# Attention with a threshold, then an MLP: the division by the softmax sums moves behind the value product, the first pairs are turned by plain transposes, and eight blocks of the MLP instead of six go through seven products of quarters

## The chip, the core and the metric

The kernel runs on one core of a Trainium2 chip. The core has a matrix engine (TensorE, PE in the profile, with its weight loads as PEld), a vector engine (VectorE, DVE), an engine for activation functions (ScalarE, ACT), GpSimd (POOL) and SyncE (SP), which here only issues transfers. Each engine works through its own list of instructions in order. Transfers are issued from SP's and POOL's lists and carried by 16 DMA engines. The metric is the device time of one execution in microseconds (us); lower is better.

## What is computed

```python
scale = 1.0 / np.sqrt(q.shape[-1])                       # q, k, v: (8, 8, 576, 64)
scores = scale * np.matmul(q, k.transpose(0, 1, 3, 2))
thresh = np.max(scores, axis=-1, keepdims=True) - tau
scores = np.where(scores >= thresh, scores, -1000000000.0)
scores = scores - np.max(scores, axis=-1, keepdims=True)
attn = np.exp(scores)
attn = attn / (np.sum(attn, axis=-1, keepdims=True) + 1e-09)
attn_out = np.matmul(attn, v)
x = attn_out.transpose(0, 2, 1, 3).reshape(8 * 576, 8 * 64)   # (4608, 512)
h = x @ w_in                                              # w_in: (512, 2048), float64
g = 0.5 * h * (1.0 + erf(h / sqrt(2)))
out = g @ w_out                                           # w_out: (2048, 512), float64
```

Everything is done in float32; the two weight matrices arrive as float64 and are converted on the chip.

## The kernel before

**Pairs, chunks and slots.** Heads are taken in pairs (e = 0, 1): 8 batches x 4 pairs are 32 pairs. The 576 rows of a head's scores are 4 chunks of 128 and a tail of 64; the tails of the two heads share a fifth chunk. One chunk of one pair is a *slot*, so a pair has five slots, i = 0 to 4, and there are 160 slots, listed in `slots` and walked by the loop at the end of the kernel. The instructions of all engines are issued in the order in which this loop calls the steps; nothing reorders them later.

**One slot.** `scores` (L345) computes 128x576 scores per head into PSUM (tile `sc`, two buffers, so each slot waits until the one before has been used). `softmax_head` takes the negated maxima (L356, DVE), the exponentials (L357, ACT) and the thresholds (L360). `softmax_tail` multiplies by "score is at least the threshold" and sums the row in one instruction (L370), adds 1e-9 and takes the reciprocal (L374, L375). For the pairs from the fifth on it then divides the weights themselves (L386 on DVE, now and then L384 on ACT).

**Turning the weights.** The value product needs the weights transposed (tile `pT`, one buffer for each of the two heads). The first four pairs (`EARLY`) use TensorE: a matmul with a diagonal matrix `diag` that holds the reciprocals (L291, made on ACT at L379), so that turning and dividing are one step. All later pairs use 32x32 transposes on DVE (`turn_p`, L398, into `pd`, or `pd_tail` in slot 4), and transfers on SP's queue put the 32x32 blocks in their places in `pT` (`regroup`): eight in slot 2 and eight in slot 3 (L413), four for the tails in slot 4 (L409).

**The value product.** `weigh_v` (L424) multiplies `pT` by `v` in two halves of 288 columns and gives 128 rows of x^T for the pair; ACT copies them from PSUM to the blocks of x^T (L433). For the later pairs it is called in slot 2 (`WEIGH`) of the next pair, between that slot's scores and its share of the MLP. The first four pairs go in two rounds (chunks 0 and 1 of all four, then chunks 2 to 4) and have it two slots after their last chunk of the round.

**The MLP.** Tokens go in 18 blocks of 256. Twelve blocks are *plain*: `block_steps` issues 64 matmuls with w_in (L473), gelus on ACT (L453), 32 matmuls with w_out (L485), the copy (L488) and the store. These are cut in small steps, and `fill` puts them behind the other steps of each slot, as many as a plan says: `GOAL` is how many blocks are to be done by which slot, and `PARTS` shares this among the five slots of a pair. The last six blocks go in three pairs (`DUOS`) through seven products of quarters in place of eight (`strassen`, matmuls at L591), after all attention work. The blocks' x^T wait in the pool `xg`; one of them (`AWAY`) is put into DRAM meanwhile (`put_away`) and fetched back (`bring`).

**Loads.** q, k and v of a pair are loaded about two pairs ahead, on SP for the first pairs and on POOL afterwards (L215, L223). In the first stage SP also loads the first pairs' q, k and v (L233 to L247). The weights are loaded by POOL in pieces, and four DVE instructions and one ACT instruction convert each piece (`conversions`, L172 to L183), between the slots' other work.

Of the kernel before, what the change touches and what calls it, by code (L numbers as in the profile page):

```python
# [18 lines left out]
def kernel(  # L19
# [28 lines left out]
    nc = tc.nc  # L48
# [19 lines left out]
    PLAIN = N_BLK - 6  # L68

    DUOS = [(n, n + 1) for n in range(PLAIN + 1, N_BLK - 1, 2)] + [(N_BLK - 1, PLAIN)]  # L70
    AWAY = [PLAIN]
# [12 lines left out]
    gp = ctx.enter_context(tc.tile_pool(name="gp", bufs=N_DF // 2 + 3))  # L84
    dg = ctx.enter_context(tc.tile_pool(name="dg", bufs=1))
# [9 lines left out]
    pd = [const.tile([P, 4 * KR, P], FP32, name=f"pd{e}") for e in range(2)]  # L95
    pd_tail = [const.tile([P, 4 * KR, Q], FP32, name=f"pd_tail{i}") for i in range(2)]
# [184 lines left out]
    def turn_p_early(p, i):  # L281


# [3 lines left out]
        w, diag = s.pop(("p", i)), s.pop(("diag", i))  # L287
        n = 1 if i == NC else 2

        def turn(to, cols, e):  # L290
            nc.tensor.matmul(to, lhsT=w[:, cols], rhs=diag[:, e, :], start=True, stop=True)  # L291

        for e in range(n):
            tr = ps.tile([P, NC, P], FP32, tag="mm", name="tr")
            for c in range(NC):
                at = e * (S + TAIL) + c * P
                turn(tr[:, c, :], slice(at, at + P), e)
            if i < NC:
                nc.scalar.copy(s["pT"][e][:, 0:NC, i * P:(i + 1) * P], tr)
# [5 lines left out]
        if i < NC:  # L305
            for e in range(2):
                at = MAIN + e * TAIL
                turn(tr[e * TAIL:(e + 1) * TAIL, 0, :], slice(at, at + TAIL), e)
            nc.scalar.copy(tails[:, i * P:(i + 1) * P], tr[:, 0, :])
            return  # L310
        turn(tr[0:TAIL, 0, :], slice(MAIN, S), 0)
# [50 lines left out]
    def softmax_tail(p, i, early, shared):  # L362

        s = st[p]
        sc, thr, w = s.pop(("sc", i)), s.pop(("thr", i)), s["p", i]
        n = len(sc)
        den = small.tile([P, 2], FP32, tag="den", name="den")
        for e in range(n):
            row = w[:, e * S:(e + 1) * S].rearrange("p (h s) -> p h s", h=2)
            nc.vector.scalar_tensor_tensor(  # L370
                row, sc[e][:, :, 0:HALF], thr[:, e:e + 1], row, op0=ALU.is_ge, op1=ALU.mult,
                accum_out=den[:, e:e + 1])
        rden = small.tile([P, 2], FP32, tag="rden", name="rden")
        nc.vector.tensor_scalar(den[:, 0:n], den[:, 0:n], 1e-9, None, op0=ALU.add)  # L374
        nc.vector.reciprocal(rden[:, 0:n], den[:, 0:n])  # L375
        if early:
            diag = s["diag", i] = dg.tile([P, 2, P], FP32, tag="diag", name="diag")
            for e in range(n):
                nc.scalar.activation(diag[:, e, :], ident, AF.Copy, bias=0.0, scale=rden[:, e:e + 1])  # L379
            return  # L380
        for e in reversed(range(n)):
            row = w[:, e * S:(e + 1) * S]
            if e == 0 and n == 2 and shared:
                nc.scalar.activation(row, row, AF.Copy, bias=0.0, scale=rden[:, e:e + 1])  # L384
            else:
                nc.vector.tensor_scalar(row, row, rden[:, e:e + 1], None, op0=ALU.mult)  # L386
# [28 lines left out]
    def weigh_v(p, lo, hi):  # L415

        b, hp = divmod(p, HP)
# [9 lines left out]
        at = lo  # L427
        while at < hi:
            n, o = divmod(b * S + at, TOK)
            size = min(TOK - o, hi - at)  # L430
            if n not in x_blk:
                x_blk[n] = xg.tile([P, N_DM, TOK], FP32, tag="x", name="x")
            nc.scalar.copy(x_blk[n][:, hp, o:o + size], xT[:, at - lo:at - lo + size])  # L433
            at += size
        if hi == S:
            del st[p]

# [122 lines left out]
    def strassen(ext, room):  # L560
# [9 lines left out]
        room += [x for _ in range(N_DF // 2 + 3) for x in unit(gp, "g")]  # L570
        room += [u for t in pd for u in units(t)]
        room += [x for e in range(2) for x in unit(one, f"pT{e}", 5)]

        def quarter():
            got = [room.pop(0).rearrange("p (j t) -> p j t", t=TOK) for _ in range(NJ // 2)]
            return lambda j: got[j // 2][:, j % 2, :]
# [143 lines left out]
    GOAL += [(BATCH * (m + 2) + WEIGH, x) for m, x in enumerate([1.96, 3.63, 5.31, 6.98, 8.65, 10.33, PLAIN])]  # L720
# [8 lines left out]
    PARTS = (1.36, 1.36, 0.5, 1.36, 0.42), (1.25, 1.25, 0.55, 1.25, 0.7)  # L729
# [4 lines left out]
    for n in range(len(slots) + WEIGH + 1):  # L734
        p, i = slots[n] if n < len(slots) else divmod(n, SLOTS)
        batch = n // BATCH
# [7 lines left out]
        busy = len(late)  # L744
# [3 lines left out]
        for args in due:  # L748
            weigh_v(*args)
        due = []  # L750
        if p > EARLY and i == WEIGH:
            for h in range(2):
                weigh_v(p - 1, h * HALF, (h + 1) * HALF)
        owed += (goal(n) - goal(n - 1)) * BLK_NS * (PARTS[n > 2 * BATCH + WEIGH][i] if not early and p < NP else 1.0)
# [6 lines left out]
        if p < NP:  # L761

            softmax_tail(p, i, early, batch == 1 and not busy)
            if not early:
                turn_p(p, i)
                if i == 2:
                    regroup(p, 1)
                if i > 2:
                    regroup(p, i)
# [72 lines left out]
```

## Time and profile before

| What | Value |
|---|---|
| time, median of 3 runs | 1446.6 us (1445.63 to 1447.43) |
| the profiled execution's own time | 1442.53 us |
| its span, first to last instruction | 1440.8 us, mean granted TensorE clock 0.992 |
| busy: PE, PEld, DVE, ACT, POOL | 1392.3, 943.3, 1036.7, 661.7, 291.2 us |
| chain that ended last, by engine | PE 84%, DVE 8%, ACT 5%, DMA 1%, issue 1% |
| DMA queue of SP (`q1`), share of 16 engines | 39.8% |
| DMA queue of POOL (`q0`), share of 16 engines | 15.0% |
| first stage (four early pairs, conversion) | 0 to about 170 us |
| pairs 4 to 31 with plain blocks between | about 170 to 1145 us |
| three pairs of blocks by seven products | 1145 to 1440.8 us |

A profile is one execution, so its rows add up to 1440.8 us and not to the median. Busy time counts an instruction from its start to its end; matmuls overlap, so the time from one start to the next tells more of PE than the mean duration. A float32 matmul has two records in the trace, a plain transpose one. An engine that is idle costs nothing unless something on the path to the end waits for it.

### The profile page before, as it was taken

The page shows a single profiled execution, that of the slowest core. Times are in us where ns is not written, and L with a number is a line of the kernel's source. Part 1 is how long each engine was busy: PE and PEld are TensorE (multiplying, and loading weights), DVE is VectorE, ACT ScalarE, POOL GpSimd, SP SyncE. Part 2 cuts the span into 40 slices and gives each one's busy share as a digit, 9 for nine tenths or more (in the row PEclk, how much of TensorE's full clock was granted, in tenths as well). Part 3 has the DMA queues.
Part 4 walks back from the last instruction along what each step waited for, and adds up shares of the span by engine and source line. Part 5 has one row for each costly group of instructions (what it writes and reads, how often), then busy time and mean ns, then how long its engine had stood idle before and what let it go on. Part 6 is the DMA issues. An engine that isn't in the chain of part 4 may idle for free.

```text
span 1440.8 us, 19431 instructions
## 1 busy us (share of the span) xinstructions
PE 1392.3 (97%) x6480; PEld 943.3 (65%) x6480; DVE 1036.7 (72%) x2344; ACT 661.7 (46%) x1122; POOL 291.2 (20%) x502
## 2 busy tenths in 40 slices
PE   6899989999999999999999999999999999999999
PEld 5576546556474656657475565756556588888887
DVE  5988889997888888788788878878877663241330
ACT  5758536536253553636355362635535241230320
POOL 3121322332222222222222222222200000000000
PEclk9999999999999999999999999999999999999999
DMA  9977367897777767666666667666644400100000
GB/s 284 269 243 200 113 122 117 137 140 126 121 121 115 130 111 119 108 122 108 115 114 114 115 107 137 107 115 115 112 96 86 89 1 0 45 1 8 23 1 30
DMA packets 421586, 156.22 MB, mean 108 GB/s; under 512 B 399984, under 2 KB 404656, under 8 KB 421488
## 3 DMA queue, kind: packets, MB, share of 16 engines
q1 hardware_dynamic: 395280, 97.82, 39.8%
q0 software_dynamic: 23808, 56.57, 15.0%
q8 instruction: 53, 0.87, 0.3%
q10 hardware_dynamic: 2400, 0.59, 0.2%
q14 instruction: 45, 0.37, 0.1%
HBM read 62.37 MB, written 9.96 MB: 50 GB/s over the span
## 4 chain that ended last, share of the span: by engine, by line
PE 84%; DVE 8%; ACT 5%; DMA 1%; issue 1%; SPq 0%; DVEq 0%; ACTq 0%
PE o_ps L485 23%; PE hT L473 20%; PE bank L591 20%; PE sc L345 11%; PE xT L424 9%; DVE nmx L356 2%; DVE p L370 2%; ACT p L357 1%; ACT L453 1%; DVE power L181 1%; PE tr L291 1%; DVE pd L398 1%; ACT L460 1%; DVE w_in L183 1%; DMA pT<-pd 1%
## 5 line engine op out<-in xcount | busy, mean ns | idle before, releaser
L357 ACT ACTIVATE p<-sc,nmx 128x576 f32<-128x576 f32 x288 | 203.0, 740 | 416.1 <-DVE nmx L356 416.1
L473 PE MATMUL hT<-x,w_in 128*128 128x256 f32 x1536 | 352.1, 383 | 0.0
L485 PE MATMUL o_ps<-w_out,g 128*128 128x512 f32 x768 | 351.4, 603 | 0.0
L473 PEld LDWEIGHTS hT<-x,w_in 128*128 128x128 f32 x1536 | 286.8, 190 | 65.8 <-issue 27.2
L356 DVE TENSOR_REDUCE nmx<-sc 128x1 f32<-128x576 f32 x288 | 205.6, 750 | 112.9 <-PE sc L345 112.4
L485 PEld LDWEIGHTS o_ps<-w_out,g 128*128 128x128 f32 x768 | 142.2, 191 | 171.5 <-issue 169.0
L370 DVE SCALAR_TENSOR_TENSOR p<-sc,thr,p 128x576 f32<-128x576 f32 x288 | 225.3, 816 | 33.5 <-ACT p L357 20.8
L215 POOL DMA_DIRECT2D q<-in_q_dram x104 | 69.8, 677 | 552.6 <-DVE q_tail L333 374.7
L424 PE MATMUL xT<-pT,v 128*64 128x288 f32 (+2 forms) x1280 | 167.5, 413 | 9.7 <-ACT g L453 9.7
L345 PE MATMUL sc<-kT,qT 64*128 64x288 f32 x960 | 158.2, 436 | 12.0 <-DVE p L370 11.6
L398 DVE STREAM_TRANSPOSE pd<-p 128x576 f32<-128x576 f32 x224 | 160.4, 753 | 1.7 <-ACT p L384 1.3
L345 PEld LDWEIGHTS sc<-kT,qT 64*128 64x128 f32 x960 | 87.5, 189 | 89.6 <-issue 70.6
L424 PEld LDWEIGHTS xT<-pT,v 128*64 128x64 f32 x1280 | 93.1, 138 | 80.7 <-issue 16.1
L386 DVE TENSOR_SCALAR p<-p,rden 128x576 f32<-128x576 f32 x240 | 120.4, 537 | 4.9
L223 POOL DMA_DIRECT2D v<-in_v_dram x208 | 110.7, 534 | 58.9 <-DMA k<-in_k_dram 34.0
L460 ACT ACT_TABLE_LOAD x72 | 92.4, 1283 | 1.3
L453 ACT ACT_TABLE_LOAD x72 | 92.4, 1283 | 1.3
L591 PE MATMUL bank<-unit 128*128 128x256 f32 x288 | 70.5, 379 | 0.0
L215 POOL DMA_DIRECT2D k<-in_k_dram x104 | 70.3, 683 | 0.0
L591 PE MATMUL bank<-x,w_in 128*128 128x256 f32 x288 | 70.0, 379 | 0.0
L591 PEld LDWEIGHTS bank<-x,w_in 128*128 128x128 f32 x288 | 54.7, 190 | 7.9 <-issue 0.5
L591 PEld LDWEIGHTS bank<-unit 128*128 128x128 f32 x288 | 54.7, 190 | 7.5
(136 smaller groups left out, 1221.0 us busy)
## 6 DMA issues: line engine op xcount, KB each, us to landing
pT<-pd SPq DMA_DIRECT2D x448, 160.0 KB, 4.8
pT<-pd_tail SPq DMA_DIRECT2D x112, 80.0 KB, 2.9
out_dram<-o_sb SPq DMA_DIRECT2D x30, 256.0 KB, 2.5
q<-in_q_dram POOLq DMA_DIRECT2D x104, 72.0 KB, 4.7
k<-in_k_dram POOLq DMA_DIRECT2D x104, 72.0 KB, 6.1
v<-in_v_dram POOLq DMA_DIRECT2D x156, 40.0 KB, 5.3
raw<-in_moe_w_out_dram POOLq DMA_DIRECT2D x10, 512.0 KB, 5.7
shifted<-in_moe_w_out_dram POOLq DMA_DIRECT2D x10, 511.5 KB, 5.7
```

Source lines behind the costliest of these rows:

```text
L215: eng.dma_start(t[e * D + f:e * D + f + Q], rows[:, :, f:f + Q])
L223: eng.dma_start(t[r:P:4, e, 0:n, :], rows[:, r * KR:r * KR + n, :])
L345: nc.tensor.matmul(sc[e][:, h, 0:HALF], lhsT=lhsT, rhs=s["kT"][rows, at:at + HALF], start=True, stop=True)
L356: nc.vector.tensor_reduce(nmx[:, e:e + 1], sc, axis=AXIS.XY, op=ALU.max, negate=True)
L357: nc.scalar.activation(w[:, e * S:(e + 1) * S].rearrange("p (h s) -> p h s", h=2), sc, AF.Exp, bias=nmx[:, e:e + 1], scale=1.0)
L370: nc.vector.scalar_tensor_tensor(row, sc[e][:, :, 0:HALF], thr[:, e:e + 1], row, op0=ALU.is_ge, op1=ALU.mult, accum_out=den[:, e:e + 1])
L386: nc.vector.tensor_scalar(row, row, rden[:, e:e + 1], None, op0=ALU.mult)
L398: nc.vector.transpose(to[:, 0:NB, :], w[:, e * S:(e + 1) * S].rearrange("p (b i) -> p b i", i=Q))
L424: nc.tensor.matmul(xT[f, 0:hi - lo], lhsT=s["v"][:, e, c, :], rhs=pT[:, c, lo:hi], start=(c == 0), stop=(c == KR - 1))
L473: nc.tensor.matmul(hT[:, j % 2, :], lhsT=w_in_sb[c][:, j * P:(j + 1) * P], rhs=x_blk[n][:, c, :], start=(c == 0), stop=(c == N_DM - 1))
L485: nc.tensor.matmul(o[:, 0:d_model], lhsT=g[j][:, m * P:(m + 1) * P], rhs=w_out_sb[j], start=(j == 0), stop=(j == N_DF - 1))
L591: nc.tensor.matmul(to, lhsT=l, rhs=r, start=start and k == 0, stop=k == len(pairs) - 1, skip_group_check=not start)
```

## The change

Three things change together.

1. *The division.* `softmax_tail` only writes the row sums, nine columns per pair, into a tile `sums`. After the last slot of a pair a new step `divisors` adds 1e-9, takes the reciprocals, turns the 128x32 tile by one 32x32 DVE transpose, stores it to DRAM and reads it back, broadcast to 64 partitions for each head, into a tile `inv` (one buffer): one store and four reads on SP's queue, ahead of the tails' `regroup`. `weigh_v` returns its last part, `divide`, which the loop calls after `softmax_tail`: DVE multiplies PSUM by `inv` into the blocks of x^T, in the place of ACT's copies. For the four early pairs the sums are stored column by column (two stores, or three with the tail) and read back with one broadcast read, once for chunks 0 and 1 and once for the rest.
2. *The turning of the early pairs.* Plain transposes with the identity take the place of the matmuls with `diag`, which is no longer made; the two tails of a chunk are turned by one.
3. *The MLP.* Ten plain blocks instead of twelve, four pairs of blocks by seven products instead of three, three blocks put away instead of one. `GOAL` and `PARTS` follow; the gelu pool has one tile less, and the work space of the products is handed out in pieces of 256 columns.

```diff
-    PLAIN = N_BLK - 6
-    DUOS = [(n, n + 1) for n in range(PLAIN + 1, N_BLK - 1, 2)] + [(N_BLK - 1, PLAIN)]
-    AWAY = [PLAIN]
+    PLAIN = N_BLK - 8
+    AWAY = [PLAIN, PLAIN + 1, PLAIN + 2]
+    last = list(range(PLAIN + 3, N_BLK)) + AWAY
+    DUOS = list(zip(last[0::2], last[1::2]))
...
-    gp = ctx.enter_context(tc.tile_pool(name="gp", bufs=N_DF // 2 + 3))
-    dg = ctx.enter_context(tc.tile_pool(name="dg", bufs=1))
+    gp = ctx.enter_context(tc.tile_pool(name="gp", bufs=N_DF // 2 + 2))
+    inv = ctx.enter_context(tc.tile_pool(name="inv", bufs=1))
...
-        def turn(to, cols, e):
-            nc.tensor.matmul(to, lhsT=w[:, cols], rhs=diag[:, e, :], start=True, stop=True)
+        def turn(to, cols):
+            nc.tensor.transpose(to, w[:, cols], ident)
...
-    def softmax_tail(p, i, early, shared):
+    def softmax_tail(p, i):
...
-                accum_out=den[:, e:e + 1])
-        rden = small.tile([P, 2], FP32, tag="rden", name="rden")
+                accum_out=sums[p % 4][:, e * NC + i:e * NC + i + 1] if i < NC else sums[p % 4][:, 2 * NC:2 * NC + 1])
+
+    def divisors(p, lo, hi):
+        s = st[p]
+        den = sums[p % 4]
+        n = 2 * NC + 1
         nc.vector.tensor_scalar(den[:, 0:n], den[:, 0:n], 1e-9, None, op0=ALU.add)
-        nc.vector.reciprocal(rden[:, 0:n], den[:, 0:n])
-        if early:
-            diag = s["diag", i] = dg.tile([P, 2, P], FP32, tag="diag", name="diag")
-            for e in range(n):
-                nc.scalar.activation(diag[:, e, :], ident, AF.Copy, bias=0.0, scale=rden[:, e:e + 1])
+        nc.vector.reciprocal(den[:, 0:n], den[:, 0:n])
+        t = s["inv", lo] = inv.tile([P, S], FP32, tag="inv", name="inv")
+        if p < EARLY:
+            rows = dram.tile([2, S], FP32, tag="rows", name="rows", bufs=4)
+            top = min(hi, NC)
+            end = S if hi > NC else top * P
+            for e in range(2):
+                nc.sync.dma_start(
+                    rows[e, lo * P:top * P].rearrange("(c i) -> i c", i=P), den[:, e * NC + lo:e * NC + top])
+            if hi > NC:
+                nc.sync.dma_start(rows[:, MAIN:S], den[:, 2 * NC:n])
+            nc.sync.dma_start(t[:, 0:end - lo * P], rows[:, lo * P:end].unsqueeze(1).to_broadcast([2, D, end - lo * P]))
             return
-        for e in reversed(range(n)):
-            row = w[:, e * S:(e + 1) * S]
-            if e == 0 and n == 2 and shared:
-                nc.scalar.activation(row, row, AF.Copy, bias=0.0, scale=rden[:, e:e + 1])
-            else:
-                nc.vector.tensor_scalar(row, row, rden[:, e:e + 1], None, op0=ALU.mult)
+        turned = small.tile([P, Q], FP32, tag="turned", name="turned", bufs=2)
+        nc.vector.transpose(turned, den)
+        rows = dram.tile([4, Q, Q], FP32, tag="turned", name="turned", bufs=4)
+        nc.sync.dma_start(rows.rearrange("a k i -> (a k) i"), turned)
+        flat = rows.rearrange("a k i -> a (k i)")
+        for e in range(2):
+            to = t[e * D:(e + 1) * D]
+            src = flat[:, e * P:(e + 1) * P].unsqueeze(0).to_broadcast([D, 4, P])
+            nc.sync.dma_start(to[:, 0:MAIN].rearrange("p (a x) -> p a x", x=P), src)
+            src = rows[2 * e:2 * e + 2, 2 * NC, :].unsqueeze(0).to_broadcast([D, 2, Q])
+            nc.sync.dma_start(to[:, MAIN:S].rearrange("p (a x) -> p a x", x=Q), src)
...
-            nc.scalar.copy(x_blk[n][:, hp, o:o + size], xT[:, at - lo:at - lo + size])
...
+        def divide():
...
+                part = slice(at - lo, at - lo + size)
+                nc.vector.tensor_tensor(x_blk[n][:, hp, o:o + size], xT[:, part], by[:, part], op=ALU.mult)
+                at += size
+        return divide
...
-    GOAL += [(BATCH * (m + 2) + WEIGH, x) for m, x in enumerate([1.96, 3.63, 5.31, 6.98, 8.65, 10.33, PLAIN])]
+    GOAL += [(BATCH * (m + 2) + WEIGH, x) for m, x in enumerate([1.96, 3.3, 4.64, 5.98, 7.32, 8.66, PLAIN])]
...
-    PARTS = (1.36, 1.36, 0.5, 1.36, 0.42), (1.25, 1.25, 0.55, 1.25, 0.7)
+    PARTS = 1.2, 1.2, 0.8, 1.2, 0.6
...
+            softmax_tail(p, i)
+        for divide in made:
+            divide()
+        if p < NP:
+            if early and i == 1:
+                divisors(p, 0, 2)
+            if i == NC:
+                divisors(p, 2 if early else 0, NC + 1)
+        if p < NP and not early:
+            turn_p(p, i)
+            if i == 2:
+                regroup(p, 1)
+            if i > 2:
+                regroup(p, i)
```

## The prediction

> **What bounds the kernel now.** I read the busy shares first, then the chain that ended last, then windows by stage, and last the timeline of SyncE's (SP's) queue against that of TensorE (PE), because the change puts transfers into that queue.
>
> ```profile
> PE 1392.3 (97%) x6480; PEld 943.3 (65%) x6480; DVE 1036.7 (72%) x2344; ACT 661.7 (46%) x1122; POOL 291.2 (20%) x502
> ```
>
> PE is busy 97% of the span, and the chain gives it 84%. The windows show that three stages differ (columns: length, then busy us and instructions of PE, weight loads, DVE, ACT, POOL, then granted clock, DMA share, GB/s):
>
> ```profile
> 0.00:170.00 170.00, 143.85 (x838) 104.01 (x838) 136.55 (x327) 117.96 (x221) 48.24 (x98) 0.95 0.78 233
> 373.00:616.98 243.98, 242.37 (x1104) 150.27 (x1104) 201.24 (x448) 121.32 (x181) 66.96 (x112) 1.00 0.70 117
> 1290.40:1387.90 97.50, 96.99 (x449) 85.06 (x449) 28.02 (x66) 25.00 (x65) 0.00 (x0) 1.00 0.03 11
> ```
>
> In the first 170 us no engine is full; VectorE (DVE) leads. In the middle PE has no gap (242 of 244 us). The last line is one pair of blocks by seven products: 97.5 us.
>
> The middle stage repeats once per pair of heads. Its hidden second cycle is the SP queue. Timeline, SP, then PE:
>
> ```profile
> 516.11 19.43 SPq L413 DMA_DIRECT2D pT<-pd  x16
> 535.64 3.17 SPq L409 DMA_DIRECT2D pT<-pd_tail  x4
> 550.75 1.39 SPq L413 DMA_DIRECT2D pT<-pd  x2
> ```
>
> ```profile
> 545.61 5.07 PE L424 MATMUL xT<-pT,v 128*64 128x288 f32 x40
> ```
>
> L424 is `weigh_v`, two halves of 2.5 us. `pT` has one buffer, so the first transfer of the next pair waits for the last matmul of `weigh_v` and starts 0.06 us after it (516.05, 550.69). Then 16 transfers are issued, then the 4 tails, and the second half of `weigh_v` (alone in reading the tail columns) can't start before they have landed. From the end of one `weigh_v`, over the 20 pairs between 344 and 1042 us, issue and landing in the trace give on average: the 16 issued by 18.9 us, landed by 22.0, the tails landed by 24.5, the second half started at 32.3. So 7.7 us of each period are slack (all 24 periods from 308.5 to 1141.3 us average 34.7). The source views of L413 (its last two issues here) and of L409 show the landing times:
>
> ```profile
> DMA to landing us min/median/max: 3.8/4.0/4.1
> DMA to landing us min/median/max: 2.4/2.7/3.1
> ```
>
> **The change part by part.**
>
> *Two blocks move to the products.* A plain block is 128 matmul records (1536 / 12) that start 0.216 us apart in the trace (L473) and 64 (768 / 12) at 0.429 (L485): 27.6 + 27.5 = 55.1 us. Two leave the middle: 110.2 us over 24 pairs is 4.6 us per pair, so PE's own work per pair falls from 34.7 to 30.1 us. The end gains one pair of blocks, +97.5. On PE's path alone: -12.7. The two further blocks put away and fetched back have 6.0 us to landing (`x<-x`); fetching lies under some 30 us of products; storing shares the DMA engines with the 16 transfers, so I put +2, not 0.
>
> *Weights no longer divided in the middle.* Per pair DVE loses 9 multiplies of 0.54 (4.8 us) and five pairs of small operations (5 x 0.34 = 1.7), and gains 1.8: four multiplies out of PSUM (two halves, each cut at a block's edge) at 0.3 (a 128x256 add from PSUM, L640, is 0.42), plus 0.55 for the sums. DVE goes from 28.5 to about 24 us per pair. It isn't the bound, so this gains nothing by itself. ACT loses the copies of L433. The divides stand behind the threshold multiply and ahead of the transposes of slot 2, so DVE now waits for the end of `weigh_v`; queued behind are 1.43 us of transposes and 1.9 of `turn_qk`. The next maxima come 4.2 us after `weigh_v`; PE reaches them after its 2.9 us of filling and 1.2 of scores, so this costs nothing.
>
> *The new transfers.* In SP's order of the changed program each pair has, between the 16 transfers and the 4 tails, a store of the turned sums to DRAM and four broadcast reads, and the first read waits for the store to land. The tails wait behind all five. Cost: the store is issued at +18.9 behind the 16, of which the last lands at +22.0; the first tail of before, in the same place, lands 3.1 to 3.9 us after its issue, so I take +22.4. Four reads at 0.57 (an early v load takes 0.52 to 0.59 to issue) end at +24.7; the tails then go out at 0.67 each, the last lands 2.45 after its issue: +29.2, against +24.5. That is 4.7 later. Bounds: 3.3 (the store landed 2.4 us after its issue as the quickest tail is, reads at 0.5) to 6.7 (landing 4.2, reads at 0.9 as with a loaded queue).
>
> Without the chain the period would be PE's 30.1, and of the slack 7.7 - 4.6 = 3.1 would be left. 4.7 is more than 3.1. So PE waits in the second half of `weigh_v`, and the cycle is the bound: 24.5 + 4.7 + 2.6 (second half) + 0.1 = about 32.0 us (30.5 to 33.9). Over 24 pairs: 24 x (34.7 - 32.0) = -65, not -110. The four pairs before them ran at 30 to 31 us with only 2 to 3.6 us of slack; they go to 32.0: +5.
>
> On this a rule of the Trainium skill bears (DMA: Bandwidth & Descriptors, "Anatomy of one DMA"): a transfer has a fixed cost of about 2.0 us, mostly the receipt of the write. Here a store behind a full queue should take 3.3 by the rows. By the page's 2.0 alone the period would be some 1.3 us shorter and the time about 31 us less.
>
> *The first pairs.* Transposes have one record per tile instead of two (L265 has 16 for 16, L291 360 for 180): twenty records of 0.12 us per chunk become nine, 1.2 us less PE per chunk. The diagonals on ACT (36 x 0.4 = 12.8 us) go. Of both I put 5 us on the path, since DVE leads there and its sum is level (twenty times 0.4 off, 3 for sums and 5 for divides on). Against that stands a new wait. The first divide is on DVE right after the multiply that ends at 37.8 us, and needs its broadcast. That transfer stands in SP's queue behind the early v loads:
>
> ```profile
> 37.05 0.81 DVE L370 SCALAR_TENSOR_TENSOR p<-sc,thr,p 128x576 f32<-128x576 f32 x1
> ```
>
> ```profile
> 46.45 0.80 SPq L247 DMA_DIRECT2D v<-in_v_dram  x1
> ```
>
> SP is done with these at 47.2 (somewhat sooner once the waiting DVE asks for no more weights); two stores at 0.5, a landing of about 2.8 (what 128 four-byte pieces of tau took), a read of about 2.8: landed near 52. Behind the waiting DVE are the maxima of the next slot and the weight conversions that lead this stage. So about 14 us are lost; the weight loads that DVE triggers pause meanwhile. Later pairs have two slots (13.5 us) for two landings of 3 to 7 us each and should fit. Net of the first stage: +9 (from -5, if the queue runs ahead, to +20, if later pairs wait too).
>
> The same skill speaks against the plain transposes (TensorE: Matmul & The Clock Gate, "PE-mode transpose"): it says they don't count as PE work for the clock. In the trace the clock is 0.89 to 1.00 here with either kind; I put nothing for it.
>
> **Sum.** 1440.8 + 97.5 - 65 + 5 + 9 + 2 = 1490 us of span. The profiled execution took 1442.5, 1.7 more than its span, and the median of the runs is 1446.6, 4.1 above that: 1490 + 5.8, about 1495 us.
>
> **The rivals.**
>
> *The chain hides* (0.13, faster). The five transfers cost less than the 3.1 us of slack that PE's 30.1 leaves. For it: DMA share is 0.70, the engines drain after +22. Then 1440.8 + 97.5 - 110 = 1428, with -5 to +2 for the first stage and 0 to 2 for the stores, plus 5.8: 1429 to 1438. It decides when they put the tails back by under 3.1; against it, even the quick bound makes 3.3.
>
> *Only the early wait counts* (0.07). The middle runs at PE's 30.1 to 30.3, the first stage loses its 9 to 14 us: 1428 + 2 + 9 to 14 + 5.8 = 1445 to 1450, no change (0.04) or a little slower (0.03).
>
> *The DMA engines fill* (0.10, slower still). The 16 transfers, POOL's loads and the new ones share engines that are busy 0.70 of 34.7 us; in 32 us that is over 0.8, landing goes to the 7 us that are seen in the rush, period 33.9 or more: 1440.8 + 97.5 - 19 + 10 + 9 + 2 + 5.8, about 1546.
>
> My forecast, the chain as the bound at about 32.0, has 0.70. The range 1442 to 1538 takes in most of the bounds of the period and of the first stage, and leaves out the faster rival and the far end of the slow one. About 0.2% is what a measurement here can tell. Faster 0.13, same 0.04, slower 0.83.
>
> **What would show it.** Right: in the changed profile PE's share falls to about 92%, and the wait list shows the matmuls of `weigh_v` waiting for `pT<-pd_tail` by about 2 us a pair; `weigh_v` recurs every 32 us; SP's line of `turned` is followed by an idle stretch of about 3.5 us; DVE waits once for over 10 us for the broadcast in the first 60 us; the last stage has four stretches of 97.5 us. Wrong: `weigh_v` every 30.1 us with PE above 96% (the chain is hidden), or DVE, not the tails, as what PE waits for; or no early wait, if the sums are stored before the v loads.

## The result, and the profile after

| | before | after |
|---|---|---|
| median of the runs on the same chip | 1446.2 us (1445.63 to 1447.43, 4 runs) | 1575.8 us (1567.83 to 1582.91, 4 runs) |
| ratio | 1 | 1.0893, 95% interval 1.0838 to 1.0948 |
| profiled execution, its span | 1442.53, 1440.8 us | 1573.56, 1571.8 us |

Slower, as forecast, but by 130 us where the forecast had 49, and outside its range (1442 to 1538). The page of after, busy shares and the chain by engine and by line:

```profile
PE 1410.9 (90%) x6348; PEld 959.6 (61%) x6348; DVE 941.3 (60%) x2078; ACT 626.4 (40%) x991; POOL 288.2 (18%) x502
...
PE 63%; DMA 19%; SPq 9%; DVE 6%; issue 2%; ACT 1%; DVEq 0%; ACTq 0%
PE bank L619 25%; PE hT L498 13%; PE o_ps L510 10%; PE sc L346 8%; PE xT L443 7%; DMA rows<-sums 6%; DMA inv<-rows 5%; DMA pT<-pd_tail 4%; SPq L431 4%; DMA turned<-turned 3%; DVE nmx L357 2%; SPq L427 2%; DVE p L369 2%; SPq L404 1%; DMA k<-in_k_dram 1%
```

PE was 97% busy and 84% of the chain; now it is 90% busy, and transfers (DMA) and SP's issuing of them (SPq) hold 28% of the chain. Two groups can be told apart by name: `rows<-sums` and `inv<-rows` (11%) belong to the first four pairs, `turned` and `pT<-pd_tail` to the later ones.

The windows of after, chosen as those of before (columns: length, busy us and instructions of PE, weight loads, DVE, ACT, POOL, then granted clock, DMA share, GB/s):

```profile
0.00:170.00 170.00, 93.53 (x466) 65.47 (x468) 96.00 (x227) 70.28 (x125) 32.96 (x69) 0.75 0.70 175
500.00:744.00 244.00, 233.76 (x1083) 144.29 (x1084) 182.97 (x397) 126.82 (x168) 69.20 (x117) 1.00 0.79 135
1178.86:1276.36 97.50, 96.99 (x448) 85.09 (x449) 39.93 (x99) 25.87 (x64) 0.00 (x0) 1.00 0.03 12
```

The last line is as forecast. In the middle PE is idle for 10.2 of 244 us, where it was idle for 1.6. The first line is the surprise: every engine does 60 to 70% of what it did in the same 170 us, and the clock is 0.75 instead of 0.95.

Two marks cut the span in three: the first regrouping transfer of pair 4 (`pT<-pd`) ends the first stage, the end of the last value product ends the middle.

| us of span | before | after | difference | forecast |
|---|---|---|---|---|
| first stage, to the first regrouping | 178.9 | 254.4 | +75.4 | +9 |
| middle, to the end of the last value product | 962.4 | 919.4 | -43.0 | -60 (-65 + 5) |
| end | 299.5 | 398.0 | +98.5 | +99.5 (97.5 + 2) |

The stages come from one profiled execution each. The sum was wrong by 82 us: 66 in the first stage, 17 in the middle, the end 1 less.

**The middle.** SP's timeline, then PE's, in the stretch that answers to the one shown of before (idle time before a row, and what ended it, in brackets):

```profile
521.54 19.27 SPq L431 DMA_DIRECT2D pT<-pd  x16
540.91 0.91 SPq L397 DMA_DIRECT2D turned<-turned  x1
543.86 0.60 SPq L402 DMA_DIRECT2D inv<-turned  x1
...
546.52 2.71 SPq L427 DMA_DIRECT2D pT<-pd_tail  x4
```

```profile
546.43 2.65 PE L443 MATMUL xT<-pT,v 128*64 128x288 f32 x20
549.97 0.67 PE L443 MATMUL xT<-pT,v 128*64 128x288 f32 x2 [0.90 <-DMA pT<-pd_tail]
551.24 2.61 PE L443 MATMUL xT<-pT,v 128*64 128x288 f32 x18 [0.59 <-issue]
```

This is the forecast mechanism, row by row: 16 transfers, the store, 2 us in which SP waits for it to land where the sign said about 3.5 (the "landing" of a transfer is the signal that it is complete, counted from the start of its issue), the reads, the tails; PE waits for the tails in the second half of `weigh_v`. The next cycle starts at 553.88: 32.3 us. The list of waits gives the tails this much of PE's time, 1.3 us for each of the 28 later pairs, where the prediction's sign said about 2:

```profile
PE xT L443 <- DMA pT<-pd_tail: 36.7, 35, 4.4
```

**The first stage.** A pair's sums go to DRAM and back as a *trip*: the stores of the columns (`rows<-sums`), then the broadcast read (`inv<-rows`). The chain, followed through the first, the third and the last trip (start, us, what):

```profile
44.86 8.62 DMA rows<-sums
53.53 5.00 DMA inv<-rows
58.62 0.42 DVE x L458
...
77.97 9.28 DMA rows<-sums
87.27 12.68 DMA inv<-rows
100.05 0.42 DVE x L458
...
226.81 18.71 DMA rows<-sums
245.65 7.24 DMA inv<-rows
```

There are eight trips (two for each of four pairs). The stores make 95.5 us of the chain and the reads 74.4, together 170 of the 254. The list of waits (us in total, times, longest), and the landing times of the stores of two columns (source view of L388):

```profile
DVE x L458 <- DMA inv<-rows: 79.2, 8, 21.6
```

```profile
DMA to landing us min/median/max: 7.8/9.0/10.8
```

DVE waits for the broadcast not once but eight times, 79.2 us in all, about what the stage has grown by. Such a store lands 9 us after its issue, where the forecast took 2.8.

### The profile page after: what moved, and what is told of

Read it like the earlier page. It is cut to its first block, busy times and chain, and to the rows that moved or that the text cites. A ratio compares the mean times of both kernels' runs of the same rounds, so it can differ in the third digit from the quotient of the medians.

```text
span 1571.8 us, 18917 instructions
## 1 busy us (share of the span) xinstructions
PE 1410.9 (90%) x6348; PEld 959.6 (61%) x6348; DVE 941.3 (60%) x2078; ACT 626.4 (40%) x991; POOL 288.2 (18%) x502
## 4 chain that ended last, share of the span: by engine, by line
PE 63%; DMA 19%; SPq 9%; DVE 6%; issue 2%; ACT 1%; DVEq 0%; ACTq 0%
PE bank L619 25%; PE hT L498 13%; PE o_ps L510 10%; PE sc L346 8%; PE xT L443 7%; DMA rows<-sums 6%; DMA inv<-rows 5%; DMA pT<-pd_tail 4%; SPq L431 4%; DMA turned<-turned 3%; DVE nmx L357 2%; SPq L427 2%; DVE p L369 2%; SPq L404 1%; DMA k<-in_k_dram 1%
## 5 line engine op out<-in xcount | busy, mean ns | idle before, releaser
L498 PE MATMUL hT<-x,w_in 128*128 128x256 f32 x1280 | 299.0, 386 | 5.0 <-DVE x L458 5.0
L510 PE MATMUL o_ps<-w_out,g 128*128 128x512 f32 x640 | 296.3, 606 | 0.0
L498 PEld LDWEIGHTS hT<-x,w_in 128*128 128x128 f32 x1280 | 240.2, 191 | 63.9 <-issue 26.3
L443 PE MATMUL xT<-pT,v 128*64 128x288 f32 (+2 forms) x1280 | 203.4, 443 | 44.1 <-DMA pT<-pd_tail 36.7
L510 PEld LDWEIGHTS o_ps<-w_out,g 128*128 128x128 f32 x640 | 117.6, 191 | 141.9 <-issue 140.1
L458 DVE TENSOR_TENSOR x<-xT,inv 128x256 f32<-128x256 f32 (+7 forms) x124 | 33.0, 307 | 192.5 <-PE xT L443 109.0
L619 PE MATMUL bank<-x,w_in 128*128 128x256 f32 x384 | 93.6, 379 | 0.5 <-ACT v L660 0.5
L619 PE MATMUL bank<-unit 128*128 128x256 f32 x352 | 87.7, 379 | 0.0
L619 PEld LDWEIGHTS bank<-x,w_in 128*128 128x128 f32 x384 | 72.9, 190 | 11.2 <-ACT v L660 0.9
L619 PE MATMUL bank<-w_out,unit 128*128 128x256 f32 x320 | 72.3, 379 | 0.0
```

The lines of the kernel that those rows point to most:

```text
L443: nc.tensor.matmul(xT[f, 0:hi - lo], lhsT=s["v"][:, e, c, :], rhs=pT[:, c, lo:hi], start=(c == 0), stop=(c == KR - 1))
L498: nc.tensor.matmul(hT[:, j % 2, :], lhsT=w_in_sb[c][:, j * P:(j + 1) * P], rhs=x_blk[n][:, c, :], start=(c == 0), stop=(c == N_DM - 1))
L510: nc.tensor.matmul(o[:, 0:d_model], lhsT=g[j][:, m * P:(m + 1) * P], rhs=w_out_sb[j], start=(j == 0), stop=(j == N_DF - 1))
L619: nc.tensor.matmul(to, lhsT=l, rhs=r, start=start and k == 0, stop=k == len(pairs) - 1, skip_group_check=not start)
```

## The experiments

Stages as in the table above; "cycle" is the mean of the 27 intervals between the ends of the value products of pairs 4 to 31 in the profiled execution. Each kernel's ratio is to runs of before on the same chip; the medians of before there were 1444.1 to 1446.2 us.

| kernel | median us | ratio to before, 95% | first | middle | cycle | end |
|---|---|---|---|---|---|---|
| before | | 1 | 178.9 | 962.4 | 34.2 | 299.5 |
| after | 1575.8 | 1.0838 to 1.0948 | 254.4 | 919.4 | 32.8 | 398.0 |
| early_diag | 1500.4 | 1.0370 to 1.0409 | 180.8 | 923.8 | 32.9 | 397.7 |
| early_rows | 1506.8 | 1.0411 to 1.0459 | 188.2 | 914.1 | 32.5 | 398.0 |
| tails_first | 1519.9 | 1.0502 to 1.0534 | 259.7 | 855.6 | 30.5 | 403.3 |
| eight_only | 1436.7 | 0.9927 to 0.9961 | 179.9 | 859.4 | 30.4 | 396.3 |
| one_store | 1569.0 | 1.0809 to 1.0900 | 251.9 | 921.9 | 32.9 | 397.9 |
| early_split | 1504.3 | 1.0371 to 1.0461 | 192.4 | 910.4 | 32.4 | 398.2 |
| diag_tails | 1437.7 | 0.9945 to 0.9973 | 178.2 | 855.7 | 30.5 | 402.0 |
| six_blocks | 1523.6 | 1.0517 to 1.0571 | 261.1 | 961.5 | 34.3 | 300.3 |
| early_plain | 1495.3 | 1.0326 to 1.0427 | 173.2 | 915.1 | 32.6 | 397.7 |
| diag_mid | 1430.0 | 0.9878 to 0.9926 | 180.9 | 848.4 | 30.2 | 398.9 |
| rows_mid | 1438.4 | 0.9941 to 0.9972 | 185.0 | 852.0 | 30.3 | 398.8 |

**early_diag: the first pairs divided and turned as before.**

```diff
-            nc.tensor.transpose(to, w[:, cols], ident)
+            nc.tensor.matmul(to, lhsT=w[:, cols], rhs=diag[:, e, :], start=True, stop=True)
...
-            if early and i == 1:
-                divisors(p, 0, 2)
-            if i == NC:
-                divisors(p, 2 if early else 0, NC + 1)
+            if not early and i == NC:
+                divisors(p, 0, NC + 1)
```

> The changed kernel, but the first four pairs are divided and turned as before: a matmul with the diagonal of the reciprocals, ACT copies x^T, no transfer of sums. The later pairs keep the divisors. Theory (the trip of the first pairs' sums through DRAM holds DVE, and with it the first stage, by some 75 us: the first regrouping transfer starts at 254.4 us instead of 178.9): it starts at about 179 us again, and the time falls by about 75 to 1500 us (1490 to 1510). Rival (the stage is long for another reason that stays, the loads or a DMA load that the new transfers of the later pairs make): it stays above 230 us and the time above 1550 us.

Measured: 1500.4 us, first regrouping at 180.8. The whole loss of the first stage goes with this step and nothing else changes (middle 923.8 against 919.4).

**early_rows: the same trip, stored in pieces of 128 bytes.**

```diff
-            rows = dram.tile([2, S], FP32, tag="rows", name="rows", bufs=4)
...
-            for e in range(2):
-                nc.sync.dma_start(
-                    rows[e, lo * P:top * P].rearrange("(c i) -> i c", i=P), den[:, e * NC + lo:e * NC + top])
...
-                nc.sync.dma_start(rows[:, MAIN:S], den[:, 2 * NC:n])
...
+            nc.vector.transpose(turned, den)
+            rows = dram.tile([Q, 4, Q], FP32, tag="rows", name="rows", bufs=4)
...
+            nc.sync.dma_start(rows.rearrange("k a i -> a k i"), turned)
...
```

> The changed kernel, but the first pairs' sums are turned by one 32x32 transpose on DVE, so that the store writes pieces of 128 bytes instead of 4; the read back is the same, with one more small one for the tails. Theory (pieces of four bytes make the store slow, 8 to 11 us a landing and two or three of them one after the other): the store lands in 3 to 4 us as that of the later pairs does (3.0), the read about 3.5 to 5 later, 8 to 10 us in all, which fit in the 13.5 us of two slots; only the first wait stays, first regrouping transfer at about 190 to 200 us, time 1575 - 60 = about 1515 us. Rival one (any small transfer lands late there, because 16 engines are 0.6 to 0.8 busy with loads): landings stay near 9 us, time 1560 to 1580. Rival two (plain transposes and their granted clock of 0.67 to 0.84 make the stage long): transposes are unchanged, so the time stays at 1575 whatever the landing does.

Measured: 1506.8 us, first regrouping at 188.2. SP's timeline of the first trip, and the only wait of DVE for such a broadcast in the first 220 us:

```profile
45.08 0.68 SPq L388 DMA_DIRECT2D rows<-turned  x1
47.13 0.56 SPq L391 DMA_DIRECT2D inv<-rows  x1
```

```profile
DVE x L460 <- DMA inv<-rows: 16.4, 1, 16.4
```

The read goes out 2.0 us after the store's issue, where it took 9.2 in after (44.29 to 53.53). One wait of 16.4 us is left. The plain transposes are still there, so they were not what made the stage long. The stage grew by 9.3 us over before: with this store, the forecast's +9 is what happens, by its own two terms: one wait (16.4 us for 14) less what the plain transposes gain.

**one_store and early_split: the number of transfers or of pieces?**

```diff
# both against early_rows
# one_store: nine columns at once, four-byte pieces, no transpose on DVE
-            nc.sync.dma_start(rows.rearrange("k a i -> a k i"), turned)
+            nc.sync.dma_start(rows.rearrange("k a i -> (a i) k")[:, 0:n], den[:, 0:n])
# early_split: four stores of 32 pieces of 128 bytes
-            nc.sync.dma_start(rows.rearrange("k a i -> a k i"), turned)
+            for a in range(4):
+                nc.sync.dma_start(rows[:, a, :], turned[a * Q:(a + 1) * Q])
```

> The changed kernel, but all nine columns of a first pair's sums are stored by one transfer in pieces of four bytes (1152 pieces of 128 partitions x 9, each time), without DVE's transpose; read back as in early_rows. Theory (the number of four-byte pieces makes the store slow; two stores of 256 pieces in flight take 8 to 11 us): 1152 pieces take about 1152 / 512 x 9 = 20 us from issue to landing, eight trips grow by 8 to 12 us each, time 1576 + 60 to 100 = 1635 to 1675 us. Rival (two or three stores instead of one are what takes long): one store lands in 3 to 4 us and the time is about 1507 us as in early_rows.

> early_rows, but the one store of the turned sums is cut into four, of 32 pieces of 128 bytes each. Theory (pieces count, not transfers): three more issues of 0.5 us, landing still 3 to 4 us, which the 13.5 us of two slots hide: 1505 to 1512 us. Rival (transfers count): four stores land later than the two of the changed kernel, 9 us or more, and the time is 1575 or above.

early_split (1504.3) says that four transfers are no dearer than one. one_store fits neither price (1635 to 1675, or 1507): 1569.0 us, as after. One store of 1152 pieces (source view of its line) lands only 2.4 us later than the median of one of 256 (9.0):

```profile
DMA to landing us min/median/max: 11.3/11.4/11.5
```

So neither the number of transfers nor, to any great degree, that of the pieces sets the time. The next two runs therefore price such a store by itself.

**probe and probe_sizes: stores on idle DMA engines.** Both are eight_only (below) with twelve extra stores in the last stage.

```diff
+            if at == 0:
+                nc.sync.dma_start(flat[0:P].rearrange("(i k) -> i k", k=1), src[:, 0:1])
+            if at == 1:
+                nc.sync.dma_start(flat[0:32 * P].rearrange("(i k) -> i k", k=32)[:, 0:1], src[:, 0:1])
...
+            if at == 8:
+                nc.sync.dma_start(flat[0:32 * P].rearrange("(i k) -> i k", k=32), src[:, 0:32])
```

> eight_only with twelve extra stores in the last stage, where the DMA engines are almost idle, three in each of the four pairs of blocks: of 128 pieces of four bytes in the first (one column), 256 in the second, 1152 in the third, and 128 pieces of 128 bytes in the fourth. They price the disputed stores by themselves. If pieces of four bytes are dear by themselves, the columns land in 7 us or more here too (256 pieces took 7.8 to 10.8 us in the changed kernel's first stage, 1152 took 11.3 to 11.5), against 2 to 3 us for the pieces of 128 bytes. If the loads of the first stage made them late, all four land within 2 to 4 us here. If time goes with the number of pieces, the three columns stand as 128 to 256 to 1152 above a start of about 2 us.

> eight_only with twelve stores of 128 or more pieces to DRAM in the last stage, now one at a time: each reads a tile that ScalarE has just written, and they are about 18 us apart. In this order: pieces of 4 bytes side by side (a column of 128); 4 bytes every 128 bytes; 4 bytes every 512 bytes; two columns (256 pieces); nine columns (1152); then 128 pieces side by side of 16, 32, 64, 128 and 512 bytes; 64 bytes every 512; 4 bytes side by side again. If a piece of four bytes is slow because it is small, all columns take about 8 us wherever they land and the time falls as the pieces grow. If it is slow because pieces of several DMA engines meet in one block of memory, the ones 128 and 512 bytes apart land in about 2 us, as the 128-byte pieces did (1.8), and the ones side by side in about 8 until the pieces fill a block. Nine columns of 1152 pieces: over 10 us by either.

In probe the three stores of each kind went out at once and queued, so it gives a single price only for the first of each: 7.9 us for 128 pieces of 4 bytes, 1.8 for 128 pieces of 128 bytes. In probe_sizes they stand alone. Source views of the first two and of the ninth store (4 bytes side by side; 4 bytes every 128 bytes; 128 bytes side by side):

```profile
L628 SPq DMA_DIRECT2D probe<-unit x1: 333/333/333, 1046.2 to 1046.2; - x1
DMA to landing us min/median/max: 7.3/7.3/7.3
```

```profile
L630 SPq DMA_DIRECT2D probe<-unit x1: 327/327/327, 1064.3 to 1064.3; - x1
DMA to landing us min/median/max: 1.4/1.4/1.4
```

```profile
L644 SPq DMA_DIRECT2D probe<-unit x1: 320/320/320, 1277.4 to 1277.4; - x1
DMA to landing us min/median/max: 1.4/1.4/1.4
```

| store of 128 partitions | us to landing |
|---|---|
| 4 bytes side by side, first and again at the end | 7.3, 7.2 |
| 4 bytes every 128 or every 512 bytes | 1.4, 1.4 |
| two columns of 4 bytes (256 pieces), nine columns (1152) | 7.6, 9.1 |
| 16, 32, 64, 128 bytes side by side | 1.4 each |
| 512 bytes side by side; 64 bytes every 512 | 1.5; 1.4 |

Of that run's forecasts the second held, but for nine columns (9.1 us, not over 10): a piece of four bytes isn't slow, pieces of four bytes next to each other are, by about 6 us, almost whatever their number (8 and 12 bytes were not tried). The windows of the first store, its first 1.3 us and the 6 us after them, show where the time lies (DMA share and GB/s are the last two columns):

```profile
1046.10:1047.40 1.30, 1.30 (x7) 1.15 (x7) 1.10 (x3) 0.78 (x3) 0.00 (x0) 1.00 0.08 7
1047.40:1053.40 6.00, 6.00 (x29) 5.28 (x29) 3.88 (x10) 2.75 (x7) 0.00 (x0) 1.00 0.00 0
```

By the packet records this store's packets are over 1.1 us after its issue, and those of the quick one (four bytes every 128) 1.0 us after theirs. The 6 us lie between the last packet and the signal of completion, while the DMA engines show no work. That pieces of different DMA engines meet in one small block of memory would explain this; what takes the 6 us isn't shown.

**tails_first: the tails ahead of the five transfers.**

```diff
-            if i == NC:
-                divisors(p, 2 if early else 0, NC + 1)
+            if early and i == NC:
+                divisors(p, 2, NC + 1)
         if p < NP and not early:
             turn_p(p, i)
...
+            if i == NC:
+                divisors(p, 0, NC + 1)
```

> The changed kernel, but for the later pairs the tails' four transfers go to SP's queue before the store and the four reads of the divisors. Theory (the five transfers ahead of the tails set the cycle of the later pairs, 32.8 us on average from one end of the value product to the next, against PE's own 30.1): the tails land some 6 us earlier, PE no longer waits for pT<-pd_tail, the cycle falls to 30.1 to 30.8, so 28 times 2.0 to 2.7 = 56 to 75 us off: 1500 to 1520 us. Rival one (the divisors come late instead: they land at about 30 us after the end of the value product, the divide that needs them stands in DVE's queue ahead of the transposes): cycle 31.5 or more, time 1540 to 1560. Rival two (the DMA engines, not the order, make the tails late): no change, 1565 to 1580.

Measured: 1519.9 us, cycle 30.5, middle 64 us shorter than in after. The wait of PE for `pT<-pd_tail` is gone from the list; DVE now waits for `inv<-turned` (30.4 us, 16 times), but only two such pieces, 7.5 us in all, are on the chain that ended last.

**eight_only: the blocks of the third part alone, on the kernel before.** `PARTS`, the gelu pool and the work space stay those of before.

```diff
-    PLAIN = N_BLK - 6
+    PLAIN = N_BLK - 8
...
-    GOAL += [(BATCH * (m + 2) + WEIGH, x) for m, x in enumerate([1.96, 3.63, 5.31, 6.98, 8.65, 10.33, PLAIN])]
+    GOAL += [(BATCH * (m + 2) + WEIGH, x) for m, x in enumerate([1.96, 3.3, 4.64, 5.98, 7.32, 8.66, PLAIN])]
```

> The kernel before, with only the third part of the change: ten plain blocks and four pairs of blocks by seven products; weights divided as before, no divisors. Theory (PE sets the cycle and the old chain of transfers hides): cycle 34.7 - 4.6 = 30.1 us, the middle 110 us shorter, the end 97.5 to 98.5 longer: 1434 to 1440 us. Rival (DVE, 28.5 us busy per pair, or the old chain, 24.5 + 2.6 us and the wait for scores, becomes the bound at about 31 to 32 us): 1446 + 98 - 24 x 3.2 = about 1467, up to 1485 us.

Measured: 1436.7 us, faster than before by 0.4 to 0.7%. PE sets the cycle at 30.4 us although DVE is 372 of 400 us busy between 500 and 900 us. The blocks pay for themselves; it is the division that costs.

**six_blocks: the first two parts, with the blocks of before.** `PARTS`, the gelu pool and the work space stay those of after.

```diff
-    PLAIN = N_BLK - 8
+    PLAIN = N_BLK - 6
...
-    GOAL += [(BATCH * (m + 2) + WEIGH, x) for m, x in enumerate([1.96, 3.3, 4.64, 5.98, 7.32, 8.66, PLAIN])]
+    GOAL += [(BATCH * (m + 2) + WEIGH, x) for m, x in enumerate([1.96, 3.63, 5.31, 6.98, 8.65, 10.33, PLAIN])]
```

> The changed kernel with twelve plain blocks and three pairs of blocks by seven products as before (its plan, GOAL, is that of before too), so the first two parts of the change without the third. Theory (the five transfers make a cycle of 32 to 33 us, which hides under PE's 34.7 us of work per pair, and cost time only where PE's work falls to 30.1): the middle is that of before within 10 us, only the first stage's 75 us stay: 1444 + 75 = about 1520 us (1512 to 1530). Rival (the transfers cost per pair whatever PE has to do): 1444 + 75 + 28 x 2.5 = 1590 us. Rival two (DVE's relief speeds up the middle): below 1505 us.

Measured: 1523.6 us. The middle is 961.5 us against 962.4 of before, with all five transfers ahead of the tails: under 34.3 us of PE's work they hide. The list of waits, whose entry in after (above) is 36.7 us, 35 times:

```profile
PE xT L442 <- DMA pT<-pd_tail: 6.4, 7, 1.5
```

**early_plain: the plain transposes alone.**

```diff
# early_diag, with
-            nc.tensor.matmul(to, lhsT=w[:, cols], rhs=diag[:, e, :], start=True, stop=True)
+            nc.tensor.transpose(to, w[:, cols], ident)
# and, for the first four pairs, no reciprocals, no diagonals and no division
```

> early_diag without the diagonals: the first four pairs are turned by plain transposes and ACT copies x^T, and the division of these four pairs is left out, so this shows the plain transposes alone. By the prediction they gain about 5 us in the first stage (20 records of TensorE per chunk become nine, ACT loses 12.8 us): first regrouping transfer at about 176 us instead of 180.8, 1495 us. Rival (plain transposes lower the granted clock of TensorE and cost what they save): 1500 us or more, with a lower clock in the first 180 us than the 0.95 of before.

Measured: 1495.3 us (1487.8 to 1504.7), first regrouping at 173.2, 7.6 us before early_diag's. Windows of the first 180 us, early_plain and then early_diag:

```profile
0.00:180.00 180.00, 147.03 (x700) 96.51 (x700) 142.14 (x313) 111.65 (x194) 49.89 (x101) 0.89 0.75 226
```

```profile
0.00:180.00 180.00, 152.70 (x871) 108.22 (x872) 142.33 (x343) 120.23 (x226) 49.88 (x101) 0.94 0.75 222
```

The clock is lower (0.89 against 0.94), as the rival has it, but PE has 171 records less and is ahead all the same in these two executions. They are the fastest of early_plain's four and the slowest of early_diag's; the medians differ by 5.1 us, and their intervals overlap, so a gain of about the forecast 5 us is likely, but not clear of noise.

**diag_tails, diag_mid, rows_mid: the parts put together.** diag_mid is diag_tails with the store ahead of the tails and the reads behind; rows_mid keeps all three parts of the change, with early_rows' store, diag_mid's order, and the v loads of pairs 2 and 3 behind the first two transfers of sums.

```diff
# diag_mid, in divisors(), for the later pairs
         nc.sync.dma_start(rows.rearrange("a k i -> (a k) i"), turned)
+        turn_p(p, NC)
+        regroup(p, NC)
         flat = rows.rearrange("a k i -> a (k i)")
# rows_mid, besides
-                load_v_early(2)
-                load_v_early(3)
...
+        if p == 0 and i == 1:
+            load_v_early(2)
+            load_v_early(3)
```

> early_diag and tails_first together: first four pairs divided by diagonals, and for the later pairs the tails ahead of the divisors' transfers. Theory (first stage and cycle add up): 1500.4 - 28 x (32.9 - 30.5) = about 1433, by the difference that tails_first made (1575.8 - 1519.9 = 56) 1444: 1430 to 1446 us, about as eight_only (1436.7), since PE bounds the middle of both at 30.4 to 30.5 us. Rival (what tails_first gained was in part a delay that the long first stage had left): over 1455 us.

> diag_tails with the store of the divisors ahead of the tails and the four reads behind them, so that the tails' issue covers the store's landing. Theory (of the five transfers, the idle wait for the store's landing and the reads cost the cycle, the store's own issue of 0.6 to 0.9 us is covered): cycle 30.4 to 30.5 us as in diag_tails, divisors land 2 to 3 us earlier, DVE waits less for them; time 1433 to 1440 us. Rival (0.9 us ahead of the tails already reaches the path): cycle over 31 us, 1455 us or more.

> All three parts of the change kept, with their transfers arranged anew: the first pairs' sums stored in pieces of 128 bytes (as early_rows), the v loads of pairs 2 and 3 behind the first two transfers of sums, and for the later pairs the store ahead of the tails and the four reads behind them (as diag_mid). Theory (the change cost time only by these transfers): DVE's first wait falls from 16.4 to 5 to 10 us and the first regrouping transfer comes at about 180 us (188.2 in early_rows, 173.2 in early_plain, which has no transfers of sums), the cycle is 30.2 us as in diag_mid: 1430 us (1424 to 1437). Rival (v of pairs 2 and 3 is late, or the first wait stays): first regrouping at 188 or later, 1438 or more; as fast as diag_mid at best.

diag_tails: 1437.7 us; the two remedies add up. diag_mid: 1430.0 us, 3 us below its forecast range and 0.7 to 1.2% under before, the best of all kernels here. Its SP timeline shows why (one cycle):

```profile
549.66 18.84 SPq L443 DMA_DIRECT2D pT<-pd  x16
568.59 0.92 SPq L407 DMA_DIRECT2D turned<-turned  x1
569.61 2.92 SPq L439 DMA_DIRECT2D pT<-pd_tail  x4
572.64 0.61 SPq L414 DMA_DIRECT2D inv<-turned  x1
```

The store lands while SP issues the tails, so the first read follows with no gap. PE is busy 399.8 of the 400 us between 500 and 900 us, at a DMA share of 0.85.

rows_mid: 1438.4 us, 0.3 to 0.6% under before, but 8 us over the forecast and over diag_mid, at about the same cycle (30.3). Its first wait of DVE is 12.3 us where 5 to 10 were expected, and the stage ends at 185.0, not 180: the store, now ahead of the v loads, still took 5 us (37.14 to 42.19) until its read went out, where the later ones of that round took 2 to 4. The rival for the first stage holds in part. The transfers explain the loss; what the first trip costs can be made smaller, but here not zero.

## Why the prediction was wrong in size

**The step that failed** is the term "+9" for the first stage, in this sentence: "Later pairs have two slots (13.5 us) for two landings of 3 to 7 us each and should fit." The first trip's store was priced with "a landing of about 2.8 (what 128 four-byte pieces of tau took)", the later landings with 3 to 7. The row of tau is a read, whose pieces are written to 128 partitions; the step is a write of four-byte pieces side by side in DRAM, for which the trace of before had no row at all. Measured: 7.3 us alone, 7.8 to 10.8 for two columns in the first stage, 8.6 to 18.7 in the chain with the two or three stores of one trip and the loads ahead of them, then 5.0 to 13.8 for the read. A trip is 21 us on average (170 / 8), not 6 to 14. And for chunks 0 and 1 each divide stands on DVE directly ahead of the next pair's `divisors`, and later trips follow on the chain by way of PE and the next scores, so a late trip delays the start of the next: eight trips in a row, 209 us from the first store (44.3) to the last divide (253.5). early_diag and early_rows show it twice: without the trips the stage is 180.8 us, with the same trips in 128-byte pieces 188.2. The prediction saw the case, "if later pairs wait too", but put it at +20 without a sum; it came at +75.

**The middle** went as forecast, with a size slightly off. The store landed 3.0 us after its issue (2.9 to 3.9; forecast 3.3 to 3.5), the reads took 0.60 each (0.57). The cycle was 32.8 us, not 32.0, inside the bounds of 30.5 to 33.9. The mis-sized term is the second half of `weigh_v`, counted as 2.6 us without a stop: over the 21 cycles between 344 and 1042 us it began 28.8 us after the end of the value product before it (forecast 29.3) and took 4.2 us on average. In the cycle shown, which took 32.3, PE stops twice in it, 0.90 us for the tails and then 0.59 us which the profile puts down to issue. What makes other cycles longer still (up to 35.8) isn't settled. PE's own 30.1 us per pair is confirmed by diag_mid (30.2), the interplay with the third part by six_blocks: the chain costs nothing on balance under 34.3 us of work, and under 30.2 it costs 75 us (923.8 of early_diag less 848.4 of diag_mid, which have the same first stage).

**What held.** The four stretches of 97.5 us and the small cost of two more blocks put away (98.5 in all). The relief of DVE as worth little by itself, where the prediction said nothing: PE sets the cycle in eight_only (30.4) and diag_mid (30.2) alike, but diag_mid's middle is 11 us shorter, half of it before the end of its first value product; whether that is the relief isn't shown. The first wait: 21.6 us in after, 16.4 in early_rows, against 14. The plain transposes and diagonals, -5 forecast, -7.6 between the profiled executions of early_plain and early_diag and -5.1 between their medians, not clear of noise; early_plain also lacks the small operations on the sums.

**The rivals.** "The chain hides" came out false with eight blocks and true with six. "Only the early wait counts" had the middle at 30.1 to 30.3 us; it ran at 32.8. "The DMA engines fill" named 1546 us, nearer than the forecast, but not by its mechanism: its cycle of 33.9 or more didn't come, and diag_mid runs at 30.2 with a larger DMA share (0.85 between 500 and 900 us, after 0.79). No rival had the wait that decided, late sums in every round of the first stage.

**The two rules.** On the Trainium skill's fixed cost of about 2.0 us (DMA: Bandwidth & Descriptors, "Anatomy of one DMA"), which that section gives for transfers issued from GpSimd, while the stores here are SyncE's: the store behind the queue took 3.0, and the price by the rows was nearer; on idle engines 1.4; the columns of four bytes 7.3, which neither the rule nor my row gave. The same page (section "Specifications") says that transfers below 512 bytes are written by read-modify-write; here pieces of 16 to 128 bytes and four-byte pieces set apart land in 1.4 us, so the size alone doesn't decide. On plain transposes that don't count for the clock (TensorE: Matmul & The Clock Gate, "PE-mode transpose"): the clock was 0.89 against 0.94 over the first 180 us, which agrees; that the fewer records saved more than this cost is likely, but not clear of noise.

## What to carry to other kernels

In these runs the price of a small store went by how its pieces lie in memory, not by its bytes: before a column is written from 128 partitions, turn it on DVE so that each partition writes a run. A round trip through DRAM that feeds an instruction in an in-order list sets the pace as soon as it is longer than the distance between its two ends (here eight trips of 21 us on average made 170 us of chain, and DVE waited for 79 of them); ask what one late trip does to the start of the next. Where a store must land before its read, put other issues of the same queue between them, and put first what the bounding engine waits for: the same five transfers cost 75 us ahead of the tails, and with the tails between the store and the reads the cycle was PE's own 30.2 us.

## What was not expected of the hardware

- Four-byte pieces side by side in DRAM, one from each of 128 partitions: 7.2 to 7.3 us to landing on idle engines; the same pieces 128 bytes apart 1.4; pieces of 16 bytes side by side 1.4. The number hardly matters: 256 pieces 7.6, 1152 pieces 9.1.
- The 6 us of such a store lie behind its packets, which are over 1.1 us after the issue.
- Such stores queue up: in probe two stores of 256 pieces issued 0.5 us apart landed 10.1 us apart, and a read of 128 rows of 4096 bytes issued behind the nine-column stores landed after 26.3 us, against 3.3 to 4.4 in eight_only.
